# A chunked linear attention and a three-way max layer on one core: chunks taken by time, an early start of the layer, and another joining of the weights

## The chip, the core and the metric

The kernel runs on one core of a Trainium2 chip. The engines named below are PE (TensorE, with its weight loads as PEld), DVE (VectorE), ACT (ScalarE), POOL (GpSimd) and SP (SyncE, which issues most DMAs). The metric is the device time of one execution in microseconds, lower is better.

## What is computed

Sizes: batch B = 4, heads H = 8, sequence S = 768, head dimension D = 48; so 3072 tokens of 384 numbers, and a hidden width of 768.

```
for t in range(S):                       # per batch and head
    cur   = outer(u * k[t], v[t])
    y[t]  = r[t] @ (state + cur)
    state = w[t][:, None] * state + outer(k[t], v[t])
x   = y as (B*S, 384)
h   = max(max(x @ w1, x @ w2), x @ w3)   # 384 -> 768
out = h @ w_out                          # 768 -> 384, float32
```

The four weight matrices arrive as 64-bit floats; the kernel gets their raw words and makes float32 numbers of them on the chip.

## The kernel before, in words

**Attention.** The sequence is cut into 24 chunks of 128 tokens. Before, chunk k is batch k // 6, time step k % 6, so six chunks of one batch follow each other through the state `sstar`. The steps of one chunk have one-letter names (the table `steps`, after L461): `n` loads its tile `tin` (decays, r, k; 678 KB), `b` scans the decays backwards (L316), `f` floors and inverts four numbers (L325, L326) and scans forwards (L327), `r` multiplies k and r by the scans (L337, L338), `c` sums squares for a later check, `d` and `e` make the diagonal of the score tile (for chunks below CS = 8 by a DVE product and eight small matmuls, later by POOL and a DVE sum; in both cases POOL writes the tile `a` by an affine select, L369), `X` is the score matmul (L387), `M` copies the masked scores into `a` (L394), `T` transposes k (L404), `U` makes the state's update (L423), `S` adds it to the state (for chunks below 8 by two identity matmuls on PE, L427, later by two DVE additions, L437) and multiplies by the decay (L439), `R` multiplies r by the state (L413), `V` the scores by v (L448), and `E` copies the result into the layer's input tile `x` and, after every fourth chunk, moves the rows of heads 6 and 7 by six DMAs (L461).

**Layer.** Four chunks make a "half" of 512 tokens, six halves in all. A half is 18 up-groups (6 column tiles f, three weights each, L144), whose PSUM tiles are taken up by ACT (first of three) and DVE (maximum, L126), and 8 down-groups (L162), 26 groups together. Half 0 runs "plain": a float32 matmul, which the trace shows as two records. Halves 1 to 5 run "split": x, h and the weights are each split in a high and a low part (ACT cast and DVE subtraction, L103 and L104), and three fp32r matmuls stand for one float32 matmul. Four PSUM tiles (`psm`) rotate.

**Weights.** There are 24 pieces of 128 by 384 numbers (18 in, 6 out), each 384 KB. `load_w` reads a piece; `split_w1` and `split_w2` make the float32 number with one ACT and four DVE instructions (L275 to L289) and check its top bits with one ACT square (L291); `split_w3` splits it (`fix`).

**Order.** All engines run in the order in which the program emits their work. Up to half 1 the string START says which comes next: a unit of attention (`a`, one sixth of a chunk), a weight (`c`), a fix (`f`), an x split (`x`) or a group (`m`); the strings FRONT, LAST, TURN and ORD give the steps within the units. From then on a loop emits one group and as many units as keep the attention one half ahead.

Of the kernel before, what the change touches and what calls it, by code (L numbers as in the profile page):

```python
# [29 lines left out]
F32 = mybir.dt.float32  # L30
F32R = mybir.dt.float32r
BF16 = mybir.dt.bfloat16
I32 = mybir.dt.int32
U32 = mybir.dt.uint32
# [8 lines left out]
NP = 4  # L43
# [16 lines left out]
UPH = UPC * CPH  # L60
NST = 3
WARM = 18
XD, LEAD = -2, 0
# [3 lines left out]
FRONT = "w U0 b1 | d1 f1 r1 | w e1 c1 S0 X1 T1 | R1 M0 | V0 E0 n3 |"  # L67
LAST = "w M0 | V0 E0 U0 W9 n3 | b1 d1 | f1 r1 w | e1 c1 S0 X1 T1 R1 |"
TURN = "b1 d1 w | f1 w | r1 c1 | e1 M0 w | "
ORD = "w R0 X1 U0 V0 E0 b2 d2 | f2 n3 w | S0 r2 c2 | e2 M1 w | T1 w | |"  # L70
# [6 lines left out]
PLAIN = 1  # L77
# [10 lines left out]
def kernel(ctx: ExitStack, tc, tin, nat, u_flat, u_pair, v_t, w_all, out, ytr):  # L88
# [3 lines left out]
        mybir.EngineType.Pool, mybir.EngineType.SP}))  # L92
    const = ctx.enter_context(tc.tile_pool(name="const", bufs=1))

    w_p = ctx.enter_context(tc.tile_pool(name="w", bufs=NW + 1))
    whi, wlo, wval = [], [], []
# [10 lines left out]
    def flush(later):  # L107
        while later:
            later.pop(0)()

    def moe_groups(x_hi, x_lo, pools, store, ends=False):

        plain = x_lo is None
        ps_m, hp, mp = pools
        h_hi, h_lo, later, behind = [], [], [], []
        top = {}

        def take_up(wi, ps):  # L120
            if wi == 0:
                top["m"] = hp.tile([128, HT], F32, name="h_hi") if plain else mp.tile([128, HT], F32, name="m")
                nc.scalar.copy(out=top["m"][:, :], in_=ps[:, :])
                return
            m = top["m"]
            nc.vector.tensor_tensor(out=m[:, :], in0=ps[:, :], in1=m[:, :], op=ALU.max)  # L126
            if wi == 2 and plain:
                h_hi.append(m)
            elif wi == 2:
                hi = hp.tile([128, HT], F32R, name="h_hi")  # L130
                lo = hp.tile([128, HT], F32R, name="h_lo")
                split(hi[:, :], lo[:, :], m[:, :], later)
                h_hi.append(hi)
                h_lo.append(lo)

        for f in range(FT):
            for wi in range(3):
                flush(later)
                ps = ps_m.tile([128, HT], F32, name="psm")
                n = 0  # L140
                for ct in range(KT):
                    terms = ((wval, x_hi),) if plain else ((whi, x_hi), (whi, x_lo), (wlo, x_hi))
                    for wt, xt in terms:
                        nc.tensor.matmul(ps[:, :], lhsT=wt[f * 3 + wi][:, ct * 128:(ct + 1) * 128], rhs=xt[:, ct, :],  # L144
                                         start=(n == 0), stop=(n == KT * len(terms) - 1))
                        n += 1
                flush(behind)
                behind.append(lambda wi=wi, ps=ps: take_up(wi, ps))
                yield
        flush(behind)  # L150
        flush(later)

        order = [(tt, f) for tt in range(CPH) for f in range(FT)]
        order.insert(FT, order.pop(FT - 1))
        pss = {}
        for n, (tt, f) in enumerate(order):
            if f == 0:
                pss[tt] = ps_m.tile([128, HT], F32, name="psm")
            tok = slice(tt * C, (tt + 1) * C)
            terms = ((h_hi, wval),) if plain else ((h_hi, whi), (h_hi, wlo), (h_lo, whi))  # L160
            for i, (ht, wt) in enumerate(terms):
                nc.tensor.matmul(pss[tt][:, 0:DM], lhsT=ht[f][:, tok], rhs=wt[FT * 3 + f][:, :],  # L162
                                 start=(f == 0 and i == 0), stop=(f == FT - 1 and i == len(terms) - 1))
            if f == FT - 1:
                o = mp.tile([128, HT], F32, name="m")[:, 0:DM]
                if ends and tt == CPH - 1:
                    nc.vector.tensor_copy(out=o[:, 0:DM // 2], in_=pss[tt][:, 0:DM // 2])
                    store(tt, o, slice(0, DM // 2), nc.sync)
                    nc.scalar.copy(out=o[:, DM // 2:DM], in_=pss[tt][:, DM // 2:DM])
                    store(tt, o, slice(DM // 2, DM), nc.scalar)  # L170
                else:
                    nc.scalar.copy(out=o, in_=pss[tt][:, 0:DM])
                    store(tt, o)
            if n % 3 == 2:
                yield

    with ExitStack() as fast:
# [23 lines left out]
        def load_nat(k):  # L201
            b, c = divmod(k, NCH)
            vt = v_p.tile([128, DM], F32, name="v")
            kr = nat_p.tile([128, 2, DM], F32, name="kr")
            if k >= CS:
                nc.sync.dma_start(out=kr[:, :, :], in_=nat[b, c, :, 1:3, :])
            nc.sync.dma_start(out=vt[:, :], in_=nat[b, c, :, 0, :])
            natt[k] = (vt, kr)

        def load(k):  # L210
            b, c = divmod(k, NCH)
# [26 lines left out]
        dec = [cst.tile([128, LINE], F32, name=f"dec{i}")[:, 0:2 * NP].rearrange("p (a b) -> p a b", a=NP) for i in range(2)]  # L238
# [4 lines left out]
        scur = cst.tile([128, NP * D], F32, name="scur")  # L243

        stage = {i: w_p.tile([128, 2, PC], F32, name="w") for i in range(NW)}

        loaded = 0

        def load_w():
            nonlocal loaded  # L250
            if loaded == NW:
                return
            i, loaded = loaded, loaded + 1
            raw = stage[i][:, :, :].rearrange("p a b -> p (a b)")
            raw = raw[:, 0:PC] if w_all.dtype == F32 else raw.bitcast(w_all.dtype)
            nc.sync.dma_start(out=raw, in_=w_all[i])
            stage[i] = raw

        def split_w1(i):

            t = stage.pop(i)
            if w_all.dtype == F32:
                wval.append(t)
                return
            if i % 2 == 0:
                pair = w_p.tile([128, 2, PC], F32, name="w")
                wval.extend(pair[:, j, :] for j in range(2))
            words = t.bitcast(U32).rearrange("p (n t) -> p n t", t=2)  # L270
            lo, hi = words[:, :, 0], words[:, :, 1]
            cv = cv_p.tile([128, lines(2 * PC)], U32, name="cv")
            top, low = cv[:, 0:PC], cv[:, PC:2 * PC]
            val = wval[i].bitcast(U32)
# [9 lines left out]
        def split_w2(i):  # L284

            if w_all.dtype == F32:
                return
# [108 lines left out]
        def goes_on(k):  # L396
            return k % NCH < NCH - 1
# [366 lines left out]
```

## Time and profile before

| | |
|---|---|
| timed runs | 446.0 us median of 3 (445.41 to 448.12) |
| profiled execution, span | 446.7 us |
| PE busy | 429.0 us (96%) |
| DVE busy | 289.1 us (65%) |
| ACT busy | 155.3 us (35%) |
| POOL busy | 61.5 us (14%) |
| DMA | 43.76 MB, mean 98 GB/s |

PE's busy share counts a matmul until its modelled end, waits within a run of matmuls included, so the share is an upper bound on its work. The span is that of the one profiled execution, 0.7 us above the median of the timed runs; the page gives no other time for it.

### The profile page before, as it was taken

The page shows a single profiled execution, that of the slowest core. Times are in us where ns is not written, and L with a number is a line of the kernel's source. Part 1 is how long each engine was busy: PE and PEld are TensorE (multiplying, and loading weights), DVE is VectorE, ACT ScalarE, POOL GpSimd, SP SyncE. Part 2 cuts the span into 40 slices and gives each one's busy share as a digit, 9 for nine tenths or more (in the row PEclk, how much of TensorE's full clock was granted, in tenths as well). Part 3 has the DMA queues.
Part 4 walks back from the last instruction along what each step waited for, and adds up shares of the span by engine and source line. Part 5 has one row for each costly group of instructions (what it writes and reads, how often), then busy time and mean ns, then how long its engine had stood idle before and what let it go on. Part 6 is the DMA issues. An engine that isn't in the chain of part 4 may idle for free.

```text
span 446.7 us, 7082 instructions
## 1 busy us (share of the span) xinstructions
PE 429.0 (96%) x2775; PEld 345.5 (77%) x2775; DVE 289.1 (65%) x517; ACT 155.3 (35%) x342; POOL 61.5 (14%) x69
## 2 busy tenths in 40 slices
PE   7898999999999999799999999999999999999993
PEld 3787564555778888698888998888988889888893
DVE  5979899898588996826477747657657634223310
ACT  1345546474345354142232332323323212312210
POOL 3010000020204020303020222022012000000000
PEclk9798899999999999899999999999999999999998
DMA  8782950830344403063303053330271000200011
GB/s 211 233 251 73 322 187 4 289 135 1 100 138 138 115 1 117 18 209 93 104 13 116 25 180 117 116 97 19 56 221 44 0 1 0 74 18 1 0 37 43
DMA packets 17388, 43.76 MB, mean 98 GB/s; under 512 B 2448, under 2 KB 8848, under 8 KB 17344
## 3 DMA queue, kind: packets, MB, share of 16 engines
q1 hardware_dynamic: 16832, 42.52, 31.1%
q10 hardware_dynamic: 512, 0.69, 0.5%
q8 instruction: 24, 0.39, 0.4%
q14 instruction: 20, 0.16, 0.1%
HBM read 37.30 MB, written 4.72 MB: 94 GB/s over the span
## 4 chain that ended last, share of the span: by engine, by line
PE 87%; DVE 8%; issue 1%; ACT 1%; SPq 1%; POOL 0%; DMA 0%; DVEq 0%; POOLq 0%; ACTq 0%
PE psm L144 51%; PE psm L162 15%; PE gram L387 5%; PE y L448 5%; PE y L413 4%; PE tu L423 2%; PE tu L404 2%; PE psm L479 1%; DVE a L394 1%; DVE gf L327 1%; DVE tin L338 1%; PE psm L362 1%; DVE gf L316 1%; PE tu L427 1%; DVE tin L337 1%
## 5 line engine op out<-in xcount | busy, mean ns | idle before, releaser
L144 PE MATMUL psm<-x_hi,w 128*128 128x512 f32 x540 | 173.0, 394 | 0.0
L144 PEld LDWEIGHTS psm<-x_hi,w 128*128 128x128 f32 x540 | 101.4, 188 | 22.7 <-issue 1.9
L144 PE MATMUL psm<-x_lo,w 128*128 128x512 f32 x270 | 105.2, 390 | 0.0
L162 PE MATMUL psm<-w,h_hi 128*128 128x384 f32 x288 | 78.5, 366 | 2.4 <-ACT h_hi L103 2.4
L126 DVE TENSOR_TENSOR m<-psm,m 128x512 f32<-128x512 f32 x60 | 41.3, 688 | 60.7 <-PE psm L144 59.9
L369 POOL TENSOR_SCALAR_AFFINE_SELECT a<-cs 128x1024 f32<-128x1024 f32 x24 | 26.6, 1108 | 257.8 <-DVE cs L366 154.3
L162 PEld LDWEIGHTS psm<-w,h_hi 128*128 128x128 f32 x288 | 52.0, 189 | 10.2 <-ACT h_hi L103 2.7
L144 PEld LDWEIGHTS psm<-x_lo,w 128*128 128x128 f32 x270 | 50.7, 188 | 9.7
L144 PE MATMUL psm<-x,w 128*128 128x512 f32 x108 | 48.0, 597 | 0.0
L457 ACT COPY x<-y 112x512 f32<-112x512 f32 x22 | 12.9, 586 | 94.0 <-PE y L448 94.0
L162 PE MATMUL psm<-w,h_lo 128*128 128x384 f32 x120 | 40.7, 339 | 0.7 <-DVE h_lo L104 0.7
L103 ACT CAST h_hi<-m 128x512 fp32r<-128x512 f32 x30 | 18.6, 622 | 57.3 <-DVE m L126 57.2
L343 ACT ACTIVATE gf<-gf 112x1034 f32<-112x1034 f32 x24 | 25.7, 1070 | 35.8 <-DVE tin L338 29.6
L144 PEld LDWEIGHTS psm<-x,w 128*128 128x128 f32 x108 | 20.1, 192 | 22.8 <-issue 21.4
L316 DVE TENSOR_TENSOR_SCAN gf<-tin,d_bwd 112x517 f32<-112x517 f32 x24 | 30.1, 1256 | 9.5 <-DMA tin<-in_tin_dram 9.5
L104 DVE TENSOR_TENSOR h_lo<-m,h_hi 128x512 fp32r<-128x512 f32 x30 | 22.6, 752 | 20.2 <-ACT h_hi L103 20.2
L327 DVE TENSOR_TENSOR_SCAN gf<-tin,d_fwd 112x517 f32<-112x517 f32 x24 | 30.8, 1282 | 0.8
L394 DVE COPY_PREDICATED a<-mask,gram 128x512 f32<-128x512 int32 x44 | 30.0, 737 | 0.9 <-PE gram L387 0.6
L387 PE MATMUL gram<-tin 48*128 48x128 f32 x352 | 26.1, 287 | 1.9 <-DVE tin L338 1.9
L104 DVE TENSOR_TENSOR x_lo<-x,x_hi 128x512 fp32r<-128x512 f32 x15 | 9.5, 688 | 26.9 <-ACT x_hi L103 26.9
L387 PEld LDWEIGHTS gram<-tin 48*128 48x128 f32 x352 | 21.7, 190 | 6.6 <-DVE tin L338 2.5
L448 PE MATMUL y<-a,v 128*48 128x128 f32 (+1 forms) x352 | 26.6, 290 | 0.0
(80 smaller groups left out, 485.1 us busy)
## 6 DMA issues: line engine op xcount, KB each, us to landing
tin<-in_tin_dram SPq DMA_DIRECT2D x23, 677.7 KB, 5.5
w<-in_w_all_dram SPq DMA_DIRECT2D x24, 384.0 KB, 6.6
kr<-in_nat_dram SPq DMA_DIRECT2D x16, 384.0 KB, 5.8
v<-in_nat_dram SPq DMA_DIRECT2D x24, 192.0 KB, 4.4
out_dram<-m SPq DMA_DIRECT2D x23, 192.0 KB, 2.1
x<-x SPq DMA_DIRECT2D x33, 32.0 KB, 1.9
tin<-in_tin_dram SPq DMA_DIRECT2D x1, 258.0 KB, 4.6
tin<-in_tin_dram ACTq DMA_DIRECT2D x1, 193.5 KB, 3.4
```

Of the source, the lines that this page charges most:

```text
L103: nc.scalar.copy(out=hi, in_=src)
L104: rest = lambda: nc.vector.tensor_tensor(out=lo, in0=src, in1=hi.bitcast(F32), op=ALU.subtract)
L126: nc.vector.tensor_tensor(out=m[:, :], in0=ps[:, :], in1=m[:, :], op=ALU.max)
L144: nc.tensor.matmul(ps[:, :], lhsT=wt[f * 3 + wi][:, ct * 128:(ct + 1) * 128], rhs=xt[:, ct, :], start=(n == 0), stop=(n == KT * len(terms) ...
L162: nc.tensor.matmul(pss[tt][:, 0:DM], lhsT=ht[f][:, tok], rhs=wt[FT * 3 + f][:, :], start=(f == 0 and i == 0), stop=(f == FT - 1 and i == l ...
L316: nc.vector.tensor_tensor_scan(out=gf[0:112, 0, ::-1], data0=t[0:112, 0:WC][:, ::-1], data1=d_bwd[0:112, ::-1], initial=0.0, op0=ALU.mult, ...
L327: nc.vector.tensor_tensor_scan(out=gf[0:112, 1, :], data0=tbuf[k % NB][0:112, 0:WC], data1=d_fwd[0:112, :], initial=0.0, op0=ALU.mult, op1 ...
L343: nc.scalar.activation(out=flat, in_=flat, func=AF.Square, accum_out=acc[0:112, k:k + 1])
L369: nc.gpsimd.affine_select(out=a[:, :, :], in_=cs[:, :].unsqueeze(2).broadcast_to([128, H, C]), pattern=[[0, H], [1, C]], compare_op=ALU.is ...
L387: nc.tensor.matmul(gs[hh][:, pr, :], lhsT=p["kp"][q:q + 48, pr, :], rhs=p["rp"][q:q + 48, pr, :], start=(pr == 0), stop=(pr == NP - 1))
L394: nc.vector.copy_predicated(out=p["a"][:, hh::2, :], mask=mask_b(NP), data=p["gs"][hh][:, :, :])
L448: nc.tensor.matmul(p["y"][q:q + m, pr, :], lhsT=natt[k][0][:, h * D:h * D + m], rhs=p["a"][:, h, :], start=(k % NCH == 0 and pr == 0), sto ...
```

## The change

Chunk k becomes time step k // 4 of batch k % 4. A half is then one time step of all four batches, and the rows of the output are stored accordingly. Each batch has its own `scur`; a new step `Z` (`decayed`) multiplies it by the decay, and `S` is an ACT copy for the first four chunks and two DVE additions after that. The identity matmuls go. `p` and `q` are the floor and the inverse as steps of their own. `r` is one multiplication of 1024 elements in place of two of 512.

A weight is made by two ACT activations (step `l`) and two DVE operations (step `c`); the source is read from two bytes further on. The check of the top bits goes to the later loop: a second read of all 24 pieces through one buffer, one piece every second group.

In half 0 the column tiles f below FR = 4 stay plain, f = 4 and 5 are split (and `FIX` fixes their weights first). Nine of its up-groups are computed as two pieces of 256 tokens: `gd` needs chunks 0 and 1, `gc` chunks 2 and 3; `ge` is a whole group. The order of everything up to the end of half 1 is written out in PARTS; `G` is an up-group of half 1, `D` and `H` are down-groups of halves 0 and 1, `t` takes up one PSUM tile, `s` is a fix, `x` an x split, `w` a load. From half 2 on the loop is as before, with the checks in it.

```diff
-            b, c = divmod(k, NCH)
+            c, b = divmod(k, B)
...
-                for hh in range(2 if k % NCH > 0 and k < CS else 0):
-                    nc.tensor.matmul(pu[0:112, 0:NP * D], lhsT=ident[0:112, 0:112], rhs=sstar[k % 2][0:112, :, hh, 0:D],
-                                     start=False, stop=True, skip_group_check=True)
...
+                if k < B:
+                    nc.scalar.copy(out=scur[k][0:112], in_=new)
+                    return
+                for hh, rows in enumerate((slice(0, 64), slice(64, 112))):
+                    nc.vector.tensor_tensor(out=scur[k % B][rows], in0=new[rows], in1=sstar[k % 2][rows, :, hh, 0:D], op=ALU.add)
+        def decayed(k):
+            nc.vector.tensor_tensor(out=sstar[k % 2][0:112, :, :, 0:D],
+                                    in0=scur[k % B][0:112].unsqueeze(2).broadcast_to([112, NP, 2, D]), ...
...
-            nc.vector.tensor_tensor(out=kp[0:112, :, :], in0=kp[0:112, :, :], in1=g3, op=ALU.mult)
-            nc.vector.tensor_tensor(out=rp[0:112, :, :], in0=rp[0:112, :, :], in1=f3, op=ALU.mult)
+            nc.vector.tensor_tensor(out=both[0:112], in0=both[0:112], in1=by[0:112], op=ALU.mult)
...
-                nc.vector.tensor_copy(out=cs[:, :], in_=ps[:, 0:H])
+                (nc.scalar.copy if k < B else nc.vector.tensor_copy)(out=cs[:, :], in_=ps[:, 0:H])
...
+        def low():
+                nc.scalar.activation(out=cv[:, 0, :], in_=head, func=AF.Relu, scale=8.0, bias=low_end[:, :])
+                nc.scalar.activation(out=cv[:, 1, :], in_=body, func=AF.Relu, scale=2.0 ** -13 * (1.0 - 1.05 * 2.0 ** -20))
...
+            nc.vector.scalar_tensor_tensor(out=cv[:, 0, :], in0=head, scalar=0x8000, in1=cv[:, 0, :],
+                                           op0=ALU.bitwise_and, op1=ALU.bitwise_or)
+            nc.vector.scalar_tensor_tensor(out=val, in0=cv[:, 0, :], scalar=16, in1=cv[:, 1, :],
+                                           op0=ALU.logical_shift_left, op1=ALU.bitwise_or)
...
+        def check_w():
+                nc.vector.tensor_scalar(out=top[:, :], in0=hi, scalar1=27, scalar2=15,
+                                        op0=ALU.logical_shift_right, op1=ALU.bitwise_and)
+                nc.scalar.activation(out=top[:, :].bitcast(F32), in_=top[:, :], func=AF.Square, bias=mid_top[:, :],
+                                     accum_out=wacc[:, i - 1:i])
+            if i < NW:
+                nc.sync.dma_start(out=again[0], in_=w_all[i])
...
-START = ("aaaaaaaaaaaaaacaaccaxmmccaacmcamfaccmaamcmcccmmamcaamc"
-         "amccamacmmcfamcmcmacamacmacmacmaffafamxmaammmaacf")
+PARTS = """R0 b0 p0 w d0 q0 e0 f0 r0 b1 w T0 p1 X0 d1 q1 U0 c0 M0 S0 f1 V0 e1 R1 r1 X1 b2 E0 p2 T1 U1 d2 n3 q2 c1 M1 S1
+           f2 n4 e2 r2 l w d3 l V1 X2 b3 E1 e3 T2 R2 c c2 M2 U2 p3 V2 c gd0 q3 l b4 E2 S2 t f3 r3 c gd1 w l X3 p4 w R3 w
...
+           ge15 c s R6 c t T6 l V6 U6 E6 p8 c7 X7 gd8 l R7 ge16 M7 t c S6 c c s t n9 T7 V7 U7 ge17 d8 E7 s s q8 t e8 D0
+           d9 n10 D1 b9 s f8 r8 D2 x D3 p9 q9 e9 s D4 D5 D6 f9 s s s Z8 D7 s r9 X8 R8 c8 b10 s s p10 S7 M8 d10 G4 G2 T8 s
...
+           n14 c12 t S11 e13 t T12 M12 t H0 Z13 H1 H2 f13 r13 H3 x H4 H5 c13 Z12 H6 H7"""
+FR = 4
...
+            if groups % 2:
+                check_w()
```

## Rows read from the trace of the kernel before

**Rows 1.** Chain that ended last: start us, duration us, engine, tile, line, records.
```profile
23.50 0.83 PE tu L427 x4
...
47.16 5.17 PE psm L144 x12
...
106.12 8.12 PE psm L162 x24
...
114.24 0.39 PE tu L404 x4
...
197.44 4.12 PE psm L144 x18
...
390.35 36.92 PE psm L144 x162
427.27 12.52 PE psm L162 x72
```

**Rows 2.** Windows: length, busy PE, PEld, DVE, ACT, POOL (instructions), clock, DMA share, GB/s.
```profile
16.00:106.00 90.00, 87.64 (x545) 57.32 (x545) 82.90 (x174) 45.32 (x109) 9.79 (x9) 0.92 0.53 169
106.10:197.40 91.30, 88.18 (x572) 71.78 (x572) 68.08 (x117) 39.82 (x90) 17.09 (x16) 0.98 0.30 88
197.40:326.00 128.60, 128.60 (x914) 111.80 (x913) 81.81 (x131) 40.47 (x85) 24.72 (x24) 1.00 0.32 95
```

**Rows 3.** The same chain, four attention pieces of one chunk in the steady part.
```profile
217.01 0.89 PE y L413 x8
217.91 1.09 PE gram L387 x16
219.00 0.54 PE tu L423 x13
219.53 0.95 PE y L448 x16
```

**Rows 4.** DVE in order of time, 25.7 to 31.5 us: start, duration, line, operation.
```profile
25.70 1.34 DVE L394 COPY_PREDICATED a<-mask,psm 128x512 f32<-128x512 int32 x2
26.93 1.22 DVE L316 TENSOR_TENSOR_SCAN gf<-tin,d_bwd 112x517 f32<-112x517 f32 x1
28.07 0.67 DVE L349 TENSOR_TENSOR kr<-tin 112x512 f32<-112x512 f32 x1
...
29.07 1.24 DVE L327 TENSOR_TENSOR_SCAN gf<-tin,d_fwd 112x517 f32<-112x517 f32 x1
30.22 0.67 DVE L337 TENSOR_TENSOR tin<-tin,gf 112x512 f32<-112x512 f32 x1
30.80 0.69 DVE L338 TENSOR_TENSOR tin<-tin,gf 112x512 f32<-112x512 f32 x1
```

**Rows 5.** DVE in order of time: one weight, and later a fix and a take-up.
```profile
35.42 0.34 DVE L276 TENSOR_SCALAR w<-w 128x384 uint32<-128x384 uint32 x1
...
35.95 0.55 DVE L280 SCALAR_TENSOR_TENSOR w<-w 128x384 uint32<-128x384 uint32 x1
36.42 0.55 DVE L289 SCALAR_TENSOR_TENSOR w<-cv,w 128x384 uint32<-128x384 uint32 x1
36.89 0.35 DVE L276 TENSOR_SCALAR w<-w 128x384 uint32<-128x384 uint32 x1
...
164.71 0.55 DVE L104 TENSOR_TENSOR w<-w 128x384 fp32r<-128x384 f32 x1
165.18 0.68 DVE L126 TENSOR_TENSOR m<-psm,m 128x512 f32<-128x512 f32 x1
165.78 1.23 DVE L316 TENSOR_TENSOR_SCAN gf<-tin,d_bwd 112x517 f32<-112x517 f32 x1
```

**Rows 6.** POOL and DVE in order of time around 43 us.
```profile
43.13 1.09 POOL L369 TENSOR_SCALAR_AFFINE_SELECT a<-cs 128x1024 f32<-128x1024 f32 x1 [10.35 <-DVE cs L364]
...
43.38 1.93 DVE L316 TENSOR_TENSOR_SCAN gf<-tin,d_bwd 112x517 f32<-112x517 f32 x1
```

**Rows 7.** All loads of the weight pieces, 24 issues, from issue to landing.
```profile
DMA to landing us min/median/max: 3.7/6.6/10.1
```

More of the change, by code (lines that the diff above doesn't have):

```diff
@@ L105, in split @@
         rest() if later is None else later.append(rest)
[L107 to L115, printed above, removed]
-        ps_m, hp, mp = pools
[L117 to L123, printed above, removed]
-                return
[L125 to L148, printed above, removed]
-                yield
[L150 to L175, printed above, removed]
@@ L506, in x_parts @@
                 split(x_hi[:, ct, :], x_lo[:, ct, :], x[:, ct, :], later)
-            flush(later)
-            return x_hi, x_lo
+            for rest in later:
+                rest()
+            return dict(all=x, hi=x_hi, lo=x_lo)
         def run(gen, n):
@@ L574, in take_x, with begin, store @@
                 xs[h] = x_parts(h)
-        def group():
-            nonlocal groups, mg
-            half = groups // GPH
-            if groups % GPH == 0:
+        def begin(half):
+            nonlocal now
+            def store(tt, o, cols=slice(0, DM), eng=nc.sync):
+                eng.dma_start(out=out[tt * S + half * C:tt * S + (half + 1) * C, cols], in_=o[:, cols])
+            up, catch_up, ups, down = moe(xs[half], pools, store, ends=half == NH - 1, plain=FR if half == 0 else 0)
+            now = dict(half=half, up=up, catch_up=catch_up, ups=ups(), down=down())
@@ new lines, in split_x, with group @@
+        def split_x():
+            h = len(xs) - (FR < FT and "hi" not in xs[0])
+            xs.setdefault(h, {}).update(x_parts(h))
+        def group(step):
+            nonlocal over
+            if step[0] in "DH":
+                next(now["down"])
+                if step == "D7":
+                    over = True
+                    free.extend(held)
+                return
+            if step[0] == "g" and not xs:
+                xs[0] = {}
+                begin(0)
+            if step[0] == "G" and now["half"] == 0:
+                begin(1)
+            if step[0] == "g":
+                xs[0].setdefault("all", xt[0])
+            at, to = PIECES[step[1]] if step[0] == "g" else PIECES["e"]
+            now["up"](int(step[1 + (step[0] == "g"):]), slice(at * C, to * C))
@@ L580, in group @@
+        warmer(WARM)
+        acts = dict(w=load_w, l=low, c=weights, s=fix, x=split_x, W=lambda: warmer(AGAIN), t=lambda: now["catch_up"](1))
+        for step in PARTS.split():
+            if step in acts:
+                acts[step]()
+            elif step[0] in "gDGH":
+                group(step)
+            else:
+                ahead(step[0], int(step[1:]))
+        groups = 2 * GPH
+        while groups < GPH * NH:
+            half, g = divmod(groups, GPH)
+            if g == 0:
                 while half not in xs:
@@ L582, in group @@
                     take_x()
[L584 to L609 removed]
+                begin(half)
+            next(now["ups" if g < 3 * FT else "down"])
+            groups += 1
+            if groups % 2:
+                check_w()
+            while units < min(UPH + groups * UPH // GPH, UNITS):
                 unit()
@@ L707, in store2 @@
                 nc.sync.dma_start(out=ot[ds(half, 1), tt * C:(tt + 1) * C, :].rearrange("h t n -> (h t) n"), in_=o)
-            for _ in moe_groups(x_hi, x_lo, pools, store2):
-                pass
+            _, _, ups, down = moe(dict(hi=x_hi, lo=x_lo), pools, store2)
+            for part in (ups, down):
+                for _ in part():
+                    pass
 def _layout(r, k, v, w, u, moe_w1, moe_w2, moe_w3, moe_w_out):
```

361 lines of the change are left out of this document (212 added, 149 removed).

## The prediction

> **What bounds the kernel now.** I read the chain that ended last first, because it says which engine sets the end, then the windows, to see where another engine is nearly as full, then DVE in order of time. In the chain the reader is to see three stretches [rows 1]. Up to 47.16 us PE has only attention to do; there the layer's first matmul starts. From there on nearly every piece is PE. Half 0's down-groups begin at 106.12, half 2 at 197.44, and the last half, alone on PE, at 390.35. In the windows [rows 2] DVE is busy 82.90 of 90.0 us (92%) between 16 and 106, but only 81.81 of 128.6 (64%) between 197.4 and 326, where PE is never idle. So the first hundred microseconds belong to PE and DVE together, the rest to PE alone: PE work saved early counts only where DVE keeps up, and DVE work moved into the later loop is covered by its 36% of idle time.
>
> **PE's work.** Rates come from chain pieces. A plain record of 512 columns takes 5.17/12 = 0.431 us, so a plain up-group (6 records) 2.59; a plain record of a down-group 8.12/24 = 0.338; a split matmul of an up-group 36.92/162 = 0.228, so nine make 2.05; of a down-group 12.52/72 = 0.174 [rows 1]. The change splits two of six column tiles of half 0: six up-groups save 0.54 each, 3.2 us, and 8 of 24 float32 down matmuls go from 0.676 to 0.522, 1.2 us. The identity matmuls go: five chunks have four records, 0.83 each [rows 1], 4.1 us. Eighteen half-width pieces have the same columns in twice as many records; I take nothing, at most half a microsecond. Attention keeps its counts (four chunks without `R`, four without `T` and `U`). PE's work falls by 8.5 us.
>
> **When the layer starts.** Walk DVE's queue. The first scan starts at the same time as now, about 4 us (it waits for the tile). A chunk costs DVE, start to start: masked copies 1.23, backward scan 1.14, product, floor and inverse together 1.00, forward scan 1.15 [rows 4]. `r` becomes one operation of 1024 elements: two starts are 0.58 apart now [rows 4], so at most 1.16; a single long one saves one start-up, at the least none, and I take 1.12. Sum 5.64. Before `gd0` stand three whole chunks (16.9), the first steps of a fourth (2.3) and two weights (1.9, below): 21 us, plus some 3 of waits for the first tile's second part and for PE's round trips, gives 28 to 29 us. PE then has `V2` behind it and the x rows of chunks 0 and 1, copied some 6 us earlier. So the layer starts some 18 us before the 47.16 of now. PE will be at half clock there, as it is in part of this stretch now (mean 0.92 from 16 to 106 [rows 2]); that costs nothing as long as DVE is late, which comes next.
>
> **Which queue decides the first two halves.** Take the last up-group of half 0, `ge17`, and add up DVE's queue ahead of it from PARTS:
> - eight chunks at 5.64 and a ninth's scan and floor (1.35): 46.5.
> - 24 weights. Now four DVE operations cost 36.89 - 35.42 = 1.47; the two left are scalar-tensor ones of the same size, 0.47 each [rows 5]: 0.94, together 22.6. ACT has two activations for one and a square, about as much.
> - take-ups: 0.60 for 512 columns [rows 5]. Five whole ones (3.0), twelve half ones at 0.34 by columns (4.1), one low part (0.6).
> - six fix subtractions at 0.47 [rows 5] (2.8), an x split of three operations (1.8), three state additions and four decays of 192 and 384 elements (about 4), small copies (0.3): 8.9.
> Sum 85.7 us. Behind `ge17` PE has: 2.05 for itself, 15.0 of half 0's down-groups (32 x 0.338 + 24 x 0.174), 36.9 and 12.5 of half 1, and attention: five `X` at 1.09, four `V` at 0.95, four `R` at 0.89, four `U` at 0.54 [rows 3], five `T` at 0.39 [rows 1], 16.9. Sum 83.4.
> Between `gd0` and `ge17` it has twelve plain and five split up-groups (31.1 + 10.3), attention of five chunks by the same rows (18.4) and four times eight small diagonal records, taken at the 0.11 of the `R` records (3.5): 63. PE alone would reach `ge17` at 28.5 + 63 = 92. DVE without a gap would at 4 + 86 = 90, with the 92% of [rows 2] at 4 + 85.7/0.92 = 97. Hence DVE is late by a little there, and 5 us of cold clock or waits on PE hide behind it.
>
> **POOL against DVE.** A scan of DVE that began while POOL wrote a diagonal took 1.93 us in place of 1.22, and ended 1.09, one scan's spacing, after POOL's end at 44.22 [rows 6]. Now the select usually falls beside the masked copies, which keep their time. In PARTS the scans, products and weight operations stand behind `e` instead. Eight selects precede `ge17`; between no more meetings than now and one each, 0 to 8 x 0.85 = 6.8 us. I take half, 3.4, since the wait lasts only as long as the rest of the select.
> The Trainium skill ("SBUF — State Buffer", section "Who interferes with whom") says that a DVE instruction with two SBUF inputs contends with a POOL instruction that reads SBUF, and that the later one blocks fully. By that rule the two-input steps, so the scans, products and weight operations, all pay, and the masked copy from PSUM does not; the trace agrees in the 1.93. With all eight paid the sum would be 438 instead of 434.
>
> So `ge17` at 4 + 89.1/0.92 = 100.8, and half 1 ends at 100.8 + 83.4 = 184.2 where it now ends at 197.4: -13.2 us. PE now idles 3.1 us between 106.1 and 197.4 and its clock dips (0.98) [rows 2]. In PARTS DVE's sum ahead of the first down-group of half 1, counted the same way, is about 142: done at 4 + 145/0.92 = 162, while PE gets there at 172, so I expect no stall in its place.
>
> **The later loop** is emitted as now from an equal state, and its PE work stays (two `R` more, 1.8 us; two `U` and two `T` less, 1.9). New are 24 checks: DVE 24 x 0.27, covered by 36% idle; ACT 24 squares, moved, not added; and 9.4 MB through SP's queue. Each waits in DVE's line for its read, which SP issues only when the check before has freed the buffer. What is queued behind is `M` and the take-ups; PE waits for those when four PSUM tiles are full, about three groups later. Two groups now last 2 x 128.6/52 = 4.95 us [rows 2]; a read takes 3.7 at best, 6.6 in the middle of a burst, 10.1 at most [rows 7], plus about 0.7 for issue and check. In the loop the reads come singly, so I take a little over 3.7, with some behind a chunk's loads: 1 us lost, from 0 to the price below. The two-byte shift of the source I price at nothing: no row shows one, and by [rows 2] DMA is at 53% in the early stretch, so even loads longer by a third fit.
>
> The last half and the tail are untouched: 446.7 - 13.2 + 1 = 434.5 for the profiled execution, and 0.7 less for the median of the runs, which stands that much below its span: **434 us**.
>
> **Rivals.**
> 1. *DVE's queue runs without gaps.* The independent batches take away the serial state, so DVE may wait less. Then the queues meet at 4 + 85.7 + 83.4 = 173, or 28.5 + 63 + 83.4 = 175 from PE's side: 446.7 - 22.4 - 0.7 = 424. For it: all waits on the state are four chunks apart. Against: semaphores and ACT's copies lie between every two steps.
> 2. *The gain is lost in PARTS.* A fixed order has no slack rule: if DVE is busy 88% of the time and pays all meetings with POOL, `ge17` comes at 4 + 92.5/0.88 = 109, half 1 ends at 192.5, and 4 us of stalls behind it bring 197: 446, no change. For it: now, too, 8% of that stretch is idle while DVE is the late engine. Against: the sum of DVE ahead is smaller by the weights alone (13 us).
> 3. *The checks set the loop's pace*, slower than before. If a read lands after 6.6 us, a round takes 7.3; 24 rounds take 175 us where 48 groups take 119, and PE, held by take-ups behind the waiting check, follows up to its three groups of lead: +56 - 6, so 484; at 5.5 us, 24 x (6.2 - 4.95) - 6 = +24: 458. It decides from a landing of about 4.3 us upwards; above 5 the gain is gone. For it: the 6.6 of [rows 7]. Against: those were issued two to five at a time, and the window's DMA share is 0.32.
>
> **How the numbers follow.** About 1% is what a measurement of this kernel can tell from no change: 441.5 to 450.5. My forecast has 0.66, with its own range 428 to 441 (POOL's price, DVE's share 0.90 to 0.96, the checks 0 to 4); rival 1 has 0.12, rival 2 0.13, rival 3 0.09. Faster takes the forecast's and rival 1's share less what reaches past 441.5: 0.76. Same 0.15, slower 0.09. The range of 8 in 10 takes in rival 1 and rival 2: 424 to 446.
>
> **What would show it.** In the changed kernel's trace the first layer matmul near 29 us; DVE's share from 16 to 106 above 0.9 and PE waiting for DVE there; the last up-group of half 0 near 101; half 2's first group near 184; no identity matmuls; check operations on DVE that wait for a landing for less than 1 us. The forecast fails if PE idles long for DVE after 30 us, if the scans beside POOL's selects all show 1.9, or if two groups of halves 2 and 3 last over 5.2 us.

## The result, and the profile after

The changed kernel takes **441.13 us** (median of 4, 439.53 to 443.62), the kernel before 445.71 (4 runs, 445.03 to 448.12): ratio 0.988 [0.983, 0.993]. Timed again in 6 runs it took 440.64 against 445.98, 0.988 [0.983, 0.994]. So 4.6 to 5.3 us are gained where 12 were forecast (446.0 to 434). The profiled execution of after took 439.53 us with a span of 437.2; it is the shortest of the four.

The chain of waits of after, in pieces that answer to [rows 1] (L164 is now an up-group's matmul, L198 a down-group's). First PE in order of time, where the layer begins and at the last up-group of half 0; then the chain.

```profile
28.54 1.78 PE L164 MATMUL psm<-x,w 128*128 128x256 f32 x7
...
97.84 0.58 PE L486 MATMUL tu<-ident,tin 112*128 112x112 f32 x4 [2.04 <-DVE scur L517]
98.35 1.09 PE L530 MATMUL y<-a,v 128*64 128x128 f32 x16
99.98 1.09 PE L505 MATMUL tu<-v,kn 128*64 128x48 f32 x16 [0.54 <-ACT kn L488]
101.00 0.80 PE L164 MATMUL psm<-x_hi,w 128*128 128x512 f32 x1
...
104.13 3.08 PE L198 MATMUL psm<-w,h_hi 128*128 128x384 f32 x10
```

```profile
110.94 1.88 DVE x_lo L130 x3
112.82 0.90 DVE d_fwd L405
...
114.84 2.04 DVE gf L411
...
117.25 2.63 DVE w L130 x2
...
128.23 6.35 PE psm L164 x27
...
187.42 4.12 PE psm L164 x18
...
380.60 36.95 PE psm L164 x162
417.55 12.52 PE psm L198 x72
```

The layer begins at 28.54 us (47.16 before), the last up-group of half 0 at 101.00, half 2 at 187.42 (197.44), the last half at 380.60 (390.35). The stretch between the last two lasts 193.2 us, before 192.9. So the whole gain is made ahead of half 2, and the chain still runs through DVE up to 128.

The windows that answer to [rows 2], cut at the same events:

```profile
16.00:101.00 85.00, 78.41 (x616) 62.72 (x616) 82.56 (x142) 51.69 (x114) 13.54 (x9) 0.95 0.58 175
101.00:187.40 86.40, 85.51 (x561) 71.48 (x561) 70.58 (x109) 33.28 (x72) 29.36 (x18) 0.99 0.34 100
187.40:318.40 131.00, 131.00 (x945) 114.18 (x944) 90.61 (x150) 55.95 (x135) 25.45 (x23) 1.00 0.52 160
```

In the first window DVE is busy 97% of the time (92% before) and PE, with its waits, 92% (97% before): DVE is now the engine that is late. POOL's busy time in the second rose from 17.09 to 29.36 us.

DVE in order of time ahead of the last up-group, and POOL in the same stretch; they answer to [rows 4 to 6]. L339 and L341 are the two joining operations of a weight, L130 a fix, L451 POOL's select, L434 and L435 two POOL products.

```profile
88.97 0.55 DVE L339 SCALAR_TENSOR_TENSOR cv<-w,cv 128x384 uint32<-128x384 uint32 x1
89.56 1.32 DVE L341 SCALAR_TENSOR_TENSOR w<-cv 128x384 uint32<-128x384 uint32 x1
90.81 1.35 DVE L130 TENSOR_TENSOR w<-w,w 128x384 fp32r<-128x384 f32 x1
92.08 1.35 DVE L339 SCALAR_TENSOR_TENSOR cv<-w,cv 128x384 uint32<-128x384 uint32 x1
...
94.61 1.35 DVE L476 COPY_PREDICATED a<-mask,gram 128x512 f32<-128x512 int32 x2
95.85 0.55 DVE L339 SCALAR_TENSOR_TENSOR cv<-w,cv 128x384 uint32<-128x384 uint32 x1
96.50 0.56 DVE L341 SCALAR_TENSOR_TENSOR w<-cv 128x384 uint32<-128x384 uint32 x1
96.98 0.72 DVE L517 TENSOR_TENSOR scur<-tu,sstar 64x192 f32<-64x192 f32 x2
```

```profile
87.98 2.50 POOL L451 TENSOR_SCALAR_AFFINE_SELECT a<-cs 128x1024 f32<-128x1024 f32 x1 [21.30 <-DVE cs L446]
90.45 1.30 POOL L434 TENSOR_TENSOR kr<-kr 128x384 f32<-128x384 f32 x1
91.82 1.19 POOL L435 TENSOR_TENSOR kr<-kr,u_bc 128x384 f32<-128x384 f32 x1
```

Three DVE operations that take 0.55 us alone take 1.32 to 1.35 beside POOL (one beside the select, two beside the products), and POOL's select takes 2.50 where 1.09 is usual. At the undisturbed weight, `L341` starts 0.65 us behind `L339`, whose result it reads; the next independent operation starts 0.48 behind it. Behind this queue stands the state addition `scur` (96.98), for which PE waits 2.04 us (97.84 above).

The checks in the later loop: how long DVE waited for their loads in all, how often, and the longest; then, of the weights' tile from 190 to 320 us, the loads from issue to landing, which answers to [rows 7].

```profile
DVE cv L360 <- DMA w<-in_w_all_dram: 14.6, 8, 3.6
```

```profile
DMA to landing us min/median/max: 2.8/3.1/5.5
```

DVE waits 14.6 us in all, eight times, so 1.8 us a time where the forecast named less than 1, but in a loop in which PE is busy without a gap (131.00 of 131.00 above).

### The profile page after: what moved, and what is told of

Same layout as the page of the kernel before. It is cut to its first block, busy times and chain, and to the rows that moved or that the text cites. A ratio compares the mean times of both kernels' runs of the same rounds, so it can differ in the third digit from the quotient of the medians.

```text
span 437.2 us, 7279 instructions
## 1 busy us (share of the span) xinstructions
PE 417.5 (95%) x2818; PEld 351.4 (80%) x2818; DVE 297.4 (68%) x486; ACT 169.6 (39%) x374; POOL 79.1 (18%) x69
## 4 chain that ended last, share of the span: by engine, by line
PE 77%; DVE 13%; issue 3%; ACT 3%; DMA 1%; SPq 1%; POOL 0%; DVEq 0%; ACTq 0%; POOLq 0%
PE psm L164 45%; PE psm L198 14%; PE gram L469 5%; PE y L530 4%; PE y L495 3%; PE tu L505 2%; DVE a L476 2%; DVE cv L339 2%; DVE gf L411 2%; PE psm L565 1%; PE tu L486 1%; DVE w L130 1%; PE psm L444 1%; DVE gf L396 1%; DVE w L341 1%
## 5 line engine op out<-in xcount | busy, mean ns | idle before, releaser
L164 PE MATMUL psm<-x_hi,w 128*128 128x512 f32 x576 | 185.5, 395 | 0.0
L164 PEld LDWEIGHTS psm<-x_hi,w 128*128 128x128 f32 x576 | 108.6, 189 | 24.0 <-issue 1.5
L164 PE MATMUL psm<-x_lo,w 128*128 128x512 f32 x288 | 112.6, 391 | 0.0
L149 DVE TENSOR_TENSOR m<-psm,m 128x512 f32<-128x512 f32 x64 | 43.8, 686 | 56.7 <-PE psm L164 56.0
L198 PE MATMUL psm<-w,h_hi 128*128 128x384 f32 x288 | 76.1, 359 | 0.0
L451 POOL TENSOR_SCALAR_AFFINE_SELECT a<-cs 128x1024 f32<-128x1024 f32 x24 | 33.6, 1400 | 228.6 <-DVE cs L448 143.0
L164 PEld LDWEIGHTS psm<-x_lo,w 128*128 128x128 f32 x288 | 54.4, 189 | 10.4
L198 PEld LDWEIGHTS psm<-w,h_hi 128*128 128x128 f32 x288 | 52.1, 188 | 5.2 <-issue 0.5
L198 PE MATMUL psm<-w,h_lo 128*128 128x384 f32 x128 | 43.0, 336 | 0.0
L130 DVE TENSOR_TENSOR h_lo<-m,h_hi 128x512 fp32r<-128x512 f32 x32 | 23.6, 741 | 19.3 <-ACT h_hi L129 19.1
L476 DVE COPY_PREDICATED a<-mask,gram 128x512 f32<-128x512 int32 x46 | 31.3, 735 | 5.2 <-PE gram L469 5.0
L164 PE MATMUL psm<-x,w 128*128 128x256 f32 (+1 forms) x126 | 33.8, 417 | 0.4 <-ACT h_hi L147 0.4
L425 ACT ACTIVATE gf<-gf 112x1034 f32<-112x1034 f32 x24 | 25.7, 1070 | 13.4 <-DVE tin L420 11.2
L420 DVE TENSOR_TENSOR tin<-tin,gf 112x1024 f32<-112x1024 f32 x24 | 30.0, 1250 | 0.5
L164 PEld LDWEIGHTS psm<-x,w 128*128 128x128 f32 x126 | 22.9, 190 | 8.0 <-issue 3.3
L434 POOL TENSOR_TENSOR kr<-kr 128x384 f32<-128x384 f32 x16 | 21.5, 1342 | 38.4 <-DMA kr<-in_nat_dram 38.2
```

The costliest lines, as they stand in the source:

```text
L130: rest = lambda: nc.vector.tensor_tensor(out=lo, in0=src, in1=hi.bitcast(F32), op=ALU.subtract)
L149: nc.vector.tensor_tensor(out=m[:, cols], in0=ps[:, cols], in1=m[:, cols], op=ALU.max)
L164: nc.tensor.matmul(ps[:, cols], lhsT=wt[i][:, ct * 128:(ct + 1) * 128], rhs=x[part][:, ct, cols], start=(n == 0), stop=(n == KT * len(term ...
L420: nc.vector.tensor_tensor(out=both[0:112], in0=both[0:112], in1=by[0:112], op=ALU.mult)
L425: nc.scalar.activation(out=flat, in_=flat, func=AF.Square, accum_out=acc[0:112, k:k + 1])
L451: nc.gpsimd.affine_select(out=a[:, :, :], in_=cs[:, :].unsqueeze(2).broadcast_to([128, H, C]), pattern=[[0, H], [1, C]], compare_op=ALU.is ...
```

## The experiments

Times are medians. Each was run beside the kernel before, whose median lay between 445.8 and 446.2; brackets give the interval of the ratio to it. Differences to after are taken from the 440.64 of its second measurement, whose single executions lay between 439.4 and 445.0.

**1. Both kernels again.**

> The changed kernel once more, unedited. Question: the two profiled executions differ by 9.5 us of span (446.7 to 437.2), the medians of the timed runs by 4.6. Theory A (the base was off): the profiled execution of the kernel before was one of its longer ones, 446.7 plus some 2.3 us around the span would be 449, above all its timed runs; ordinary runs of it have spans near 443, ordinary runs of the changed kernel near 439, and the ratio stays at 0.985 to 0.992. Theory B (the first measurement was unlucky for the change): the medians now differ by about 9 us, ratio 0.980 or less.

> The kernel before, unedited, profiled a second time. Theory A expects a span of 442 to 445, half 2's first up-group at 193 to 196 instead of 197.4, and the difference in the granted clock or the waits of the first 50 us or around 170 to 190 us. Theory B expects 446 to 447 with the same milestones (47 us, 106 us, 197 us, 390 us).

After: 440.64, ratio 0.988, as theory A had it. Its profiled execution has a span of 438.7; the layer begins at 31.3 us and half 2 at 189.0. Before: one execution of 446.0 us with a span of 444.3; the layer begins at 44.5, half 2 at 194.9. The chain's pieces where half 2 begins, in after and in before:

```profile
189.02 4.12 PE psm L164 x18
```

```profile
194.91 4.12 PE psm L144 x18
```

Thus the execution from which the forecast was made (span 446.7) was some 2.4 us longer than this one, all of it ahead of 47 us, and the device time is the span plus 1.7 us (before) to 2.3 (after), not the span less 0.7.

**2. The check of the weights, left out, and put back where it was.** The first computes no check at all:

```diff
-            while wide and len(again) <= NW:
-                check_w()
```

> The changed kernel without the check of the weights' top bits and its second read (left out: 24 reads, 24 DVE shifts, 24 ACT squares, and their part of the final verdict). If the later loop hides the checks, as the prediction took (1 us), the time stays within 1.5 us of the changed kernel's (439 to 441) and half 2's first group to half 5's first group stays at 193 us. If the checks are where the gain went, the time falls by 4 us or more, to 437 or below, and that stretch to 189 or less.

439.53, 0.985 [0.979, 0.990]; half 2 to the last half 192.7 us against 193.2 in after. By that stretch the checks cost 0.5 us; the medians lie 1.1 apart, no more than executions of one kernel differ. Rival 3 falls.

```diff
+            top = cv[:, 0, :]
+            nc.vector.tensor_scalar(out=top, in0=head, scalar1=11, scalar2=15, op0=..., op1=ALU.bitwise_and)
+            nc.scalar.activation(out=top.bitcast(F32), in_=top, func=AF.Square, ...)
```

> The changed kernel with the check of the top bits done beside the joining, as the kernel before does it (one DVE shift of 0.27 to 0.35 us and one ACT square of 0.8 us more per weight before the end of half 0), and no second read. If DVE's queue sets the last up-group of half 0, as the prediction says, that group comes 24 x 0.27 to 0.35 = 6.5 to 8.4 us later than at 101 us, and the time rises by 5 to 8 us, to 446 or more. If PE or the weights' arrival sets it, the group moves by less than 2 us and the time stays within 2 us.

460.78, 1.032 [1.026, 1.038]: 20 us slower, far more than 24 shifts. ACT's square waits for DVE's shift, and behind it in ACT's line stand the activations that make the inputs of DVE's next joins (total us, times, longest):

```profile
ACT cv L346 <- DVE cv L344: 27.5, 18, 3.8
```

So half 0's down-groups begin at 125.9 us in place of 104.1 and 105.7 (the two traces of after). That moving the check out of the weights is worth its second read is shown; the size is that of this placing.

**3. Does DVE set the first hundred microseconds?** One more DVE shift per weight, whose result nobody reads:

```diff
+            nc.vector.tensor_scalar(out=cv[:, 0, :], in0=head, scalar1=11, scalar2=15, ...)
```

> The changed kernel with one DVE operation more per weight (the shift of the top bits, result unused), nothing more on ACT. The run with the whole check in place lost 20 us, more than the DVE sum of 8; ACT stood idle there 27.5 us waiting for the shift. Theory DVE: DVE is busy 97% of the time until the last up-group of half 0 (ge17, 101 us), so 24 operations of 0.27 to 0.45 us move that group and the end by 6.5 to 11 us: 447 to 452. Rival ACT: ACT's own line set the 20 us, and DVE has room: less than 3 us, 441 to 444.

448.33, 1.005 [1.002, 1.008]: +7.7 us, and half 2 at 197.1. Each of the 24 added operations (0.36 us long, about 0.28 from start to start) moves the end by some 0.32 us, so by about its own length: DVE sets it.

**4. POOL beside DVE.** The select twice for the first eight chunks; as a control a memset of the same tile, which writes as much and reads nothing:

```diff
+            if k < CS:   # b2
+                nc.gpsimd.affine_select(out=a[:, :, :], in_=cs[:, :].unsqueeze(2).broadcast_to([128, H, C]), ...)
...
+            if k < CS:   # b3
+                nc.gpsimd.memset(a[:, :, :], 0.0)
```

> The changed kernel with POOL's select of the first eight chunks done twice in a row (the same tile, the same values; POOL reads the eight sums from SBUF again). In the changed kernel's trace eight DVE operations before ge17 took 0.7 to 0.9 us longer beside a select, 6.3 us in all. Theory (DVE operations with two SBUF inputs wait for a POOL operation that reads SBUF): eight more meetings of up to 1.1 us each, half 0's down-groups 4 to 9 us later, time 444 to 450. Rival (only the tile's lateness counts, or POOL's second operation runs beside DVE): under 2 us, as in the memset control.

> Control for the doubled select: POOL fills the same tile by a memset ahead of its select, for the first eight chunks; it writes as many elements and delays the tile as long, but reads nothing from SBUF. Theory (only reads contend): DVE's operations beside the memset keep their durations, time within 2 us of the changed kernel (439 to 443). If writing contends too, or the tile's lateness costs, 444 to 450 as for the doubled select.

The second select: 447.91, 1.002 [0.999, 1.005], +7.3 us. The memset: 441.34, 0.989 [0.983, 0.995], no cost beyond the spread. The mean of the second joining operation ahead of the last up-group, in after and with the second select:

```profile
L341 DVE SCALAR_TENSOR_TENSOR w<-cv 128x384 uint32<-128x384 uint32 x24 | 15.6, 651 | 2.1
```

```profile
L341 DVE SCALAR_TENSOR_TENSOR w<-cv 128x384 uint32<-128x384 uint32 x24 | 18.4, 768 | 2.1
```

Ahead of half 0's down-groups 15 DVE operations are longer by 0.6 to 0.9 us, 11.5 us together; in after they are nine (the expectation counted eight) with 7.0. That is 4.5 of the 7.3 us. The rest can be the tile's lateness, for which DVE waits here (total us, times, longest; in the two traces of after 0 and 0.9):

```profile
DVE a L480 <- POOL a L455: 3.0, 2, 2.1
```

The memset is no control for this lateness: it runs while POOL is idle, before the select's input is there, and delays no tile. What it does show is how long DVE's operations take beside a write, here the last of the eight and the two joining operations:

```profile
80.15 0.99 POOL L452 MEMSET a<- 128x1024 f32 x1 [11.57 <-PE y L532]
```

```profile
80.16 0.55 DVE L339 SCALAR_TENSOR_TENSOR cv<-w,cv 128x384 uint32<-128x384 uint32 x1
80.75 0.56 DVE L341 SCALAR_TENSOR_TENSOR w<-cv 128x384 uint32<-128x384 uint32 x1
```

All DVE operations that begin beside the eight memsets keep their usual durations. It is POOL's reading that stops DVE, not its writing. The Trainium skill ("SBUF — State Buffer", section "Who interferes with whom") says just this, that a DVE instruction with two SBUF inputs contends with a POOL instruction that reads SBUF and not with one that only writes it; the durations in the two runs agree. An operation with one input was held too: the floor of 112x4 (L405) takes 0.88 us beside a select in place of 0.17.

**5. The dependent pair.** The second joining operation of a weight is issued behind the next operation on DVE (the code that says when `second` is called is left out):

```diff
-            nc.vector.scalar_tensor_tensor(out=val, in0=cv[:, 0, :], ...)
+            second()
+            second_of.append(lambda: nc.vector.scalar_tensor_tensor(out=val, in0=cv[:, 0, :], ...))
```

> The changed kernel with the second joining operation of a weight put one DVE operation later wherever the written order lets it, so that it no longer follows directly on the first, whose result it reads. In the changed kernel's trace the second starts 0.57 to 0.66 us after the first, other neighbours of that size 0.47 apart; 24 such pairs are some 4 us of DVE before 101 us. Theory (a wait for the result just written, on the engine that sets ge17): ge17 and the end 2 to 4 us earlier, 437 to 439. Rival (the spacing belongs to the operation itself, or PE sets ge17 by then): within 1 us of the changed kernel.

**436.16**, 0.976 [0.972, 0.980]: 4.5 us faster than after, the fastest kernel of this study. In its trace (`L342` is the second operation) 9 of the 24 pairs still stand together, as at 54.95, and 15 are apart; behind an operation that it does not need, the second starts 0.47 later (95.17 and 96.10):

```profile
54.95 0.55 DVE L339 SCALAR_TENSOR_TENSOR cv<-w,cv 128x384 uint32<-128x384 uint32 x1
55.61 0.56 DVE L342 SCALAR_TENSOR_TENSOR w<-cv 128x384 uint32<-128x384 uint32 x1
...
94.69 0.56 DVE L339 SCALAR_TENSOR_TENSOR cv<-w,cv 128x384 uint32<-128x384 uint32 x1
95.17 0.55 DVE L342 SCALAR_TENSOR_TENSOR w<-cv 128x384 uint32<-128x384 uint32 x1
95.64 0.55 DVE L339 SCALAR_TENSOR_TENSOR cv<-w,cv 128x384 uint32<-128x384 uint32 x1
96.10 0.55 DVE L342 SCALAR_TENSOR_TENSOR w<-cv 128x384 uint32<-128x384 uint32 x1
```

So the spacing does not belong to the operation itself. The 15 pairs are worth some 2.7 us (15 x 0.18). The rest of the 4.5 is not separated; the new order also brings the state addition `scur` forward, for which PE waits 0.28 us here in place of 2.04. Nor is it the reading alone that costs: in the kernel before, `L289` reads what `L280` has just written and starts 0.47 behind it [rows 5]. There the trace has no wait of DVE for itself at that place; in after every `L341` waits for the semaphore that `L339` raises, and starts 0.56 to 0.59 us behind it when that is its only wait, 0.63 to 0.67 when a second one comes with it. The Trainium skill ("VectorE: DVE Perf Modes", section "The DRAIN you can't avoid") says that a semaphore behind every one of eight copies cost nothing extra; in this trace an operation that waits for the one just ahead starts later by 0.09 to 0.20 us, and here the measurement decides.

On top of it, the selects of chunks 4 to 7 moved in PARTS to stand beside the masked copies:

> The kernel with the second joining operation later (436.2), and the diagonals of chunks 4 to 7 moved ahead, so that POOL's select begins as DVE begins the masked copies of the chunk before, whose scores come from PSUM. Theory (a DVE operation with two SBUF inputs waits for POOL's select, masked copies don't, DVE sets ge17): four meetings of 0.8 us fall away, 2 to 3.5 us less, 433 to 434.5. Rival (PE sets ge17 by now, or the diagonals' matmuls hold DVE up): 435.5 or more.

438.12, 0.983 [0.982, 0.984], 2 us slower: the theory is not confirmed. The meetings did fall, from 6.2 us of lengthened DVE operations to 4.2. But between 30 and 100 us DVE now waits for the diagonals' matmuls, the second half of the rival (total us, times, longest):

```profile
DVE cs L457 <- PE psm L455: 4.0, 3, 2.0
```

**6. The forecast's PE savings.** The kernel before without its identity matmuls; the changed kernel with no group ahead of its four chunks; and without split column tiles in half 0:

```diff
-                for hh in range(2 if k % NCH > 0 and k < CS else 0):   # c1, on the kernel before
-                    nc.tensor.matmul(pu[0:112, 0:NP * D], lhsT=ident[0:112, 0:112], ...)
-                if k % NCH > 0 and k >= CS:
+                if k % NCH > 0:
...
-... gd0 ... gd1 ... gd2 ... gd3 gc2 ... gc1 ...   # c2, PARTS
+... ge2 ... ge1 ...
...
-FR = 4   # c3
+FR = 6
```

> The kernel before with one part of the change alone: the identity matmuls gone, the state added by two DVE operations for every chunk. The prediction counted 4.1 us of PE work saved. Theory (DVE and the serial chain set the first 100 us): the saving is hidden, and five pairs of additions (0.7 us each) come onto DVE; time within 2 us of the kernel before (444 to 448). Rival (PE work counts everywhere): 4 us less, 442 or below.

> The changed kernel with the pieces of 256 tokens undone: each of the nine up-groups of half 0 is computed whole, where its later piece stood, with one take-up. DVE's sum hardly changes (12 half take-ups of 0.34 become 6 of 0.6). If DVE alone sets ge17, whenever PE starts, the time stays within 1.5 us (439 to 442). If the early start is needed, PE begins near 45 us with 63 us of work ahead of ge17, reaches it at 107 to 110 instead of 101, and the time rises by 6 to 9 us, to 446 to 450.

> The changed kernel with all six column tiles of half 0 plain (no x split for half 0, its two low parts gone, the first fixes moved a little later). PE has 4.4 us more (six up-groups at 0.54, eight down matmul pairs at 0.15), DVE some 3 us less before ge17. Theory (DVE sets ge17): the later PE work of ge17 and the down-groups adds 1.8 us, DVE gives back about as much; time within 2 us of the changed kernel (439 to 443). Rival (PE's sum is what counts): 4 us or more, 444.5 or above.

c1: 449.67, 1.007 [1.003, 1.010], 3.9 us slower, beyond both expectations. c2: 442.85, 0.993 [0.991, 0.995], 2.2 us above after, between the theories, but with executions (441.5 to 445.6) that overlap those of after: with the layer at 47.6 us in place of some 30, the end moves by about 2 us at most. c3: 436.9, 0.980 [0.978, 0.981], 3.7 us *faster* than after, though PE has 4.4 us more to do; neither expectation had that. Two of these three parts of the change cost time by themselves, the identity matmuls' removal in the kernel before and the split in the changed one.

**7. Turned round in the changed kernel.** The identity matmuls back for chunks 4 to 7, with an ACT copy in place of the DVE additions; and combinations:

```diff
+                for hh in range(2 if B <= k < CS else 0):
+                    nc.tensor.matmul(pu[0:112, 0:NP * D], lhsT=ident[0:112, 0:112], ...)
-                if k < B:
-                    nc.scalar.copy(out=scur[k][0:112], in_=new)
+                if k < CS:
+                    nc.scalar.copy(out=scur[k % B][0:112], in_=new)
```

> The changed kernel with identity matmuls again for chunks 4 to 7, and ACT copies in place of the DVE additions. Theory, DVE sets the first 100 us: three additions of some 0.45 us leave DVE's queue ahead of the last up-group, 1 to 1.4 us, and PE's 3.3 us more of matmuls hide ahead of it but for the one chunk behind it (0.83): 440.6 - 0.5 = 440, from 437.5 to 441. Rival, the forecast's sum (PE work counts in full): 440.6 + 3.3 = 444.

> Two edits that each took time away, together: the second joining operation of a weight behind another operation (436.2 alone) and no split column tile in half 0 (436.9 alone). Theory, DVE sets the first 100 us: both shorten DVE's queue ahead of the last up-group (24 dependent pairs at 0.17 = 4.1 us; six fix subtractions at 0.47 and the double take-ups), so they add, as long as PE isn't the later one: 440.6 - 4.5 - 3.7 = 432.4, with half 2 starting near 181. Rival, PE is the later one by now: the plain up-groups cost PE 4.4 us more, so nothing is added, 436 to 438.

> Second join later, no split in half 0, and the identity matmuls back for chunks 4 to 7. Theory, DVE still the later one: the effect of the identity matmuls alone on top of d1, 432 less 0 to 1 us. Rival, with DVE's queue 8 us shorter PE is the later one: PE's 3.3 us count, 435 to 436.

d2: 436.95, 0.979 [0.974, 0.984], 3.7 us faster: more than the theory's sum, which left out that PE waits for the additions behind DVE's whole line (the 2.04 us above; no such wait is in d2's trace). d1: 438.7, 0.981 [0.978, 0.985]: nothing is added to c3's 436.9 (the intervals overlap), as the rival had it, and it is 2.5 us above the later join alone (436.16). d3: 441.27, 0.988 [0.984, 0.992], above what either expectation named and 2.6 us above d1, where the rival had 3.3 for the identity matmuls. Busy time of PE, PEld, DVE, ACT and POOL from 30 to 100 us, in after, with the later join alone, in d2, d1 and d3:

```profile
30.00:100.00 70.00, 64.79 (x476) 50.62 (x474) 67.86 (x120) 42.99 (x95) 8.76 (x6) 1.00 0.59 182
```

```profile
30.00:100.00 70.00, 67.89 (x503) 54.52 (x503) 68.53 (x127) 44.27 (x97) 10.01 (x6) 0.99 0.57 176
```

```profile
30.00:100.00 70.00, 69.49 (x519) 55.96 (x516) 67.36 (x117) 44.94 (x99) 8.79 (x6) 0.99 0.57 181
```

```profile
30.00:100.00 70.00, 69.47 (x491) 51.47 (x489) 65.93 (x119) 41.65 (x93) 9.89 (x6) 0.98 0.58 184
```

```profile
30.00:100.00 70.00, 69.47 (x470) 51.62 (x467) 62.89 (x110) 41.69 (x94) 9.85 (x6) 0.98 0.56 183
```

In after PE has 5 us to spare and DVE 2 (3.3 and 2.8 in the second trace of after). The later join, which adds nothing to PE, leaves PE 2.1; the two reliefs that hand work back to PE leave it 0.5 (d2) and 0.25 (c3). With two or three together (d1, d3) DVE is the one that has time left, 4 and 7 us, and most of PE's longer work is paid: d1 adds 4.4 us of PE work to the later join, of which 2.1 would fit, and is 2.5 us slower; d3 adds 3.3 more and costs 2.6. One relief gave 3.7 to 4.5 us and none of the combinations that were run added to it: the two engines lie about 4 us apart, and the gain of one edit ends where the other engine takes over. The later join with the identity matmuls alone, and those with c3 alone, were not run.

## Where the forecast held, and which of its steps failed

Two steps failed, the base of the sum and PE's stretch behind the last up-group; a third, DVE's queue, came out by luck.

**The start of the layer** (28 to 29 us): 28.54 in the profiled execution. In four more traces whose work is the same up to there (after again, no check, the memset, the identity matmuls back; the memset is more work for POOL alone) it lies at 28.8 to 31.6, so the ordinary start is nearer to 31. The half clock that was expected there is not in this execution (granted clock 1.00 from 28.5 to 32), but it is in the second one (0.50 from 29.0 to 31.3).

**DVE's queue up to the last up-group** (100.8): 101.00, and 102.9 in the second trace. The sum came out although three of its terms did not. The second operation of a weight was priced at 0.47 like `L289` of before; it starts 0.56 to 0.67 behind the first, some 4 us more for 24. POOL's meetings were priced at 3.4 us; nine operations of DVE ahead of 101 are longer by 0.7 to 0.9 us each, 7.0 together (three are shown above), two of them beside POOL's products, which were not counted. Other terms came out lower, some 3 us together, half of it in product, floor and inverse (some 0.8 a chunk in place of 1.00): start to start the queue is some 94 us long in place of 89.1. Against these 5 us stands DVE's share, taken at 92% from the trace of before; it is 97% (rival 1 argued that batches in turn leave fewer waits; no run tests that, and an operation that POOL lengthens counts as busy). The terms were wrong and their sum right by luck.

**PE behind it** (83.4, "I expect no stall in its place"): 187.4 - 101.0 = 86.4. This step failed; in the second trace it is 189.02 - 102.86 = 86.2. The last up-group itself takes 3.13 us where 2.05 were taken: PE had waited for DVE up to 97.8 and for ACT's copy of k up to 100.0, and its records take 0.80 and 0.63 us at first, where 0.39 is usual; the mean granted clock from 101.0 to 104.1 is 0.66, between the two levels of 1.2 and 2.4 GHz (0.50 and 1.00 here). In d2, where the wait for DVE is gone, the same group takes 2.20 us at a clock of 1.00; with the later join, where PE waits 0.28 us for DVE and 1.29 for ACT, it takes 2.19 at 1.00. That the waits bring the clock down is likely, but no run shows it by itself. Of the other 1.9 us some 1.1 lie between 104 and 128, 0.9 of them idle time of PE, where the chain still runs through DVE: scans and fixes beside POOL's products (2.04 and 2.63 us above). From 128 on PE is never idle; the last 0.8 are up-group records that follow each other after 0.233 us in place of 0.228. The estimate that DVE would be ahead by 10 us over the whole of half 1 was an average; in the first fourth of it DVE was behind.

**The later loop** (+1 for the checks): +0.3 in the profiled execution, and 0.5 by the stretch of experiment 2. Right. The loads landed after 3.1 us in the middle, where 3.7 to 6.6 were feared. The sign that was named for it, waits of less than 1 us, was not met; the waits of 1.8 us did not reach PE.

**PE's 8.5 us.** They were right as work and wrong as a gain. Ahead of the last up-group DVE was known to be late, and there the identity matmuls and the split column tiles trade PE time for DVE time (additions, fixes, an x split). The forecast priced that DVE time in its queue but never asked what the change would be without these two parts. Experiments 6 and 7: each of them, turned round alone, gives 3.7 us.

**The base** ("446.7 - 13.2 + 1 = 434.5 for the profiled execution, and 0.7 less for the median of the runs, which stands that much below its span"). This step failed most. The device time is 1.7 to 2.3 us *above* the span, and the profiled execution of before was a long one by 2.4. Of the 7.3 us between that sum (433.8) and 441.1, about 3.0 come from this (437.2 + 2.3 instead of - 0.7), 2.7 from the span (437.2 against 434.5, the 3.0 behind the last up-group less the cheaper loop), and 1.6 from the profiled execution being the shortest of its four. Taken from an ordinary execution of before, 444.3, to an ordinary one of after, 438.7, the span fell by 5.6 where 12.2 were forecast. Of the 6.6 that are missing, 2.4 were in the long execution of before alone, 2.1 come from the last up-group at 102.9 in place of 100.8, 2.8 from PE behind it (86.2 in place of 83.4), and the loop gives 0.6 back. Why single executions of the same code begin the layer 2 to 3 us apart stays open.

**The rivals.** The first (DVE without gaps) was right about the gaps and wrong about the time, since the queue itself was longer. The second (the gain lost in PARTS) named the right place, behind the last up-group, with 4 us of stalls; 3 us were lost there, about 1 of them stalls. The third fell.

## What to carry to other kernels

Where two engines are equally late, price an edit that moves work from one to the other on both, and look at what the kernel would be without it: two parts here that saved PE 8.5 us cost time, and turning round either one alone gave 3.7 us back; with the later join beside it, the split turned round gave nothing and the identity matmuls cost 2.6. Take the price of an operation that waits for the one just ahead from a pair that does wait, and look at what reads beside it; moving 15 of 24 such operations back in the line was worth 4.5 us. Look in the trace, too, at when a control does its work: the memset fell into idle time. And compare the profiled execution's stages with a second execution before taking its span as the base of a sum.

## What the hardware showed that was not expected

A DVE operation of 128x384 that waits for the semaphore of the one just ahead starts 0.56 to 0.67 us after it in after; without that wait such operations start 0.47 apart, in before even when they read the result just written. POOL and DVE slow each other: the select's mean is 1.40 us over after's 24 against 1.09 alone, with one at 2.50, and DVE's operations 1.3 instead of 0.55; beside a POOL memset of the same tile DVE's operations keep their 0.55. The start of the kernel varies from execution to execution at the same code: the layer began at 28.5 in one of after and 31.3 in another, and the four executions of the first measurement had spans from 437.2 to 441.3 and mean granted clocks from 0.985 down to 0.969.
